# Turning q, k and alpha on VectorE instead of TensorE in a gated linear attention kernel

## The chip, the cores and the metric

The kernel runs on one core of a Trainium2 chip. The metric is the device time of one execution in microseconds (us). One run of the kernel before, at 390.9 us, was left out as slow. Engines are named as in the profile: PE is TensorE's matmuls, PEld its weight loads, DVE is VectorE, ACT is ScalarE, POOL is GpSimd, SP is SyncE; a "q" behind a name (SPq, ACTq) is that engine's sequencer, which issues the DMAs. "L102" is a line of the kernel's source.

## The reference

Two recurrences, one behind the other, all in fp32:

```python
# attention: batch 4, heads 8, steps S = 768, head width D = 48
for t in range(S):
    state = alpha[:, :, t, :, None] * state + einsum('bhd,bhe->bhde', k[:, :, t], v[:, :, t])
    y[:, :, t] = einsum('bhd,bhde->bhe', q[:, :, t], state)
x = y.transpose(0, 2, 1, 3).reshape(B, S, H * D)          # (4, 768, 384)

# gated state-space layer: d_model 384, d_inner 512
val, gate = split(x @ w_in)
for t in range(S):
    h = exp(A_log) * h + val[:, t, :]
    ys[:, t, :] = h
out = (silu(gate) * ys) @ w_out
```

## The kernel before

The kernel works in 12 groups n of 256 steps, three to a batch entry. The program of a group is cut into generators (`front` for the decays and scores, `back` for the attention output, `ssm` for the layer behind it), whose steps are dealt out by hand, so that TensorE works on group n's front, group n-1's back and group n-2's and n-3's layer in turn. In the timelines shown here each engine takes its instructions in that order.

Alpha, q and k arrive with the steps on the partitions. The recurrence is written with cumulative products of alpha along the steps, so all three must stand the other way round, channels on partitions and steps along the row. TensorE turns them, 128x128 at a time, into PSUM (`turned`):

```python
def front(n):
    ...
    def turned(name, jj):
        tp = ps_tp.tile([C, 2, GC], FP32, tag="tp", name="tp")
        for u in range(2):
            j = 2 * jj + u
            for c in range(G):
                nc.tensor.transpose(tp[:, u, ds(c * C, C)], pad[name][:, c, 2 * j:2 * j + 2, :], ident)
        return tp

    for jj in range(NP // 2):                  # alpha: scans V (backwards) and P (forwards)
        tp = turned("a", jj)
        ...
            nc.vector.tensor_tensor_scan(out=V[:, 2 * jj + u, GC - 1::-1], data0=tp[:, u, ::-1], ...)
        nc.vector.reciprocal(iV0[:, js], V[:, js, 0])
            nc.vector.tensor_tensor_scan(out=P[:, 2 * jj + u, :], data0=tp[:, u, :], ...)
    junk = p1.tile([C, NP, GC], FP32, name="junk")      # two range checks of V, on ScalarE
    nc.scalar.activation(junk, V[:, :, 0:GC], AF.Relu, ..., accum_out=left[:, n, 0:1])
    nc.scalar.activation(junk, V[:, :, 0:GC], AF.Relu, ..., accum_out=left[:, n, 1:2])
    yield
    ...     nc.vector.tensor_mul(Q[:, js], turned("q", jj), P[:, js])
    yield
    ...     nc.vector.tensor_mul(K[:, js], turned("k", jj), V[:, js, 1:GC + 1])
    yield
    ...     # scores sc = K.T Q on TensorE, masked into A by copy_predicated
```

The layer's two kinds of PSUM tile share two buffers (one tag), and the output copies are on ScalarE, behind the range checks in its order:

```python
def ssm(n, xT, prev_h, pool, ps_mm):           # ps_mm: 2 buffers
    for cc in range(NI):
        pj = ps_mm.tile([C, 2, GC], FP32, tag="mm", name="pj")
        ...                                     # pj = w_in.T xT; scan hh; sg = silu; f = sg * hh
        yield
    for c in range(G):
        o = ps_mm.tile([C, DM], FP32, tag="mm", name="o")
        ...                                     # o = f.T w_out
        nc.scalar.activation(o_sb, o, AF.Copy)
        nc.sync.dma_start(out=out[b, ds(g * GC + c * C, C), :], in_=o_sb)
        yield
```

A general version for data outside the range that the checks allow follows in the program; it is not taken for these inputs.

Of the kernel before, what the change touches and what calls it, by code (L numbers as in the profile page):

```python
# [10 lines left out]
U8 = mybir.dt.uint8  # L11
# [7 lines left out]
def kernel(  # L19
# [58 lines left out]
    def load_heads(dst, src, n, queue=nc.sync):  # L78

        b, g = divmod(n, NG)  # L80
        for c in range(G):
            rows = ds(g * GC + c * C, C)
            queue.dma_start(out=dst[:, c, :, 0:D], in_=src[b, :, rows, :].rearrange("h p d -> p h d"))  # L83

    def ssm(n, xT, prev_h, pool, ps_mm):
# [18 lines left out]
# [3 lines that stand above are left out]
                nc.tensor.matmul(o, f[:, cc, ds(c * C, C)], w_out[:, cc, :],  # L107
                                 start=(cc == 0), stop=(cc == NI - 1))
            o_sb = pool.tile([C, DM], FP32, name="o_sb")
            nc.scalar.activation(o_sb, o, AF.Copy)  # L110
            nc.sync.dma_start(out=out[b, ds(g * GC + c * C, C), :], in_=o_sb)
            yield
# [9 lines left out]
    def block_states(Kn, v_sb, pool, tag):  # L122

        z = pool.tile([C, NR, 512], FP32, tag=tag, name="z")
        zv = z[:, :, 0:GP * D].rearrange("p r (g j e) -> p r g j e", g=G, e=D)
        for g in range(G):
            for j in range(NP):
                for r in range(NR):
                    for i in range(2):
                        rows, chs = ds(R * r, R), ds(DP * i, DP)  # L130
                        nc.tensor.matmul(zv[chs, r, g, j, :], Kn[rows, g, j, chs],  # L131
                                         v_sb[rows, g, 2 * j + i, :], start=True, stop=True,
                                         skip_group_check=True)
        return zv

    def values_inside(A, v_sb, ps_y, pool, turn):
# [4 lines left out]
        for c in range(G):  # L141
            for j in range(NP):
                for r in range(NR):
                    for i in range(2):
                        rows, at = ds(R * r, R), ds(R * ((r + turn * i) % NR), R)
                        nc.tensor.matmul(yv[at, i, c, j, :], A[rows, i, c * NP + j, :],  # L146
                                         v_sb[rows, c, 2 * j + i, :],
                                         start=(c == 0 and j == 0), stop=False, skip_group_check=True)
# [32 lines left out]
    def ranged(ctx):  # L181
# [7 lines left out]
        wst = pool("wst", 1)  # L189
# [8 lines left out]
        pads = [{n: own.tile([C, G, H, DP], FP32, name=f"{n}_pad{i}") for n in "aqk"} for i in range(NBUF)]  # L198

        def clear_pads(i, name):  # L200
            nc.gpsimd.memset(pads[i][name][:, :, :, D:DP], 1.0 if name == "a" else 0.0)
# [3 lines left out]
        def load(n, names="aqkv", queue=nc.sync):  # L205
            for name in names:
                if name == "v":
                    vs[n] = p3.tile([C, G, H, D], FP32, name="v_sb")
                dst = vs[n] if name == "v" else pads[n % NBUF][name]
                load_heads(dst, dict(a=alpha, q=q, k=k, v=v)[name], n, queue)  # L210
# [10 lines left out]
        words, scales = [], {}  # L221

        def fetch_unit(u, queue=nc.sync):
            dst, src = units[u]
            m, w = dst.shape[1:]
            bits = wst.tile([C, m, w, 2], U32, name=f"bits{u}")
# [51 lines left out]
        def front(n):  # L278

            pad = pads[n % NBUF]  # L280
            V = Vs[n % 2]
            iV0 = p2.tile([C, NP], FP32, name="iV0")
            P = p1.tile([C, NP, GC], FP32, name="P")
            Q = p3.tile([C, NP, GC], FP32, name="Q")
            K = p2.tile([C, NP, GC], FP32, name="K")
# [4 lines left out]
            def turned(name, jj):  # L290
                tp = ps_tp.tile([C, 2, GC], FP32, tag="tp", name="tp")
                for u in range(2):
                    j = 2 * jj + u
                    for c in range(G):
                        nc.tensor.transpose(tp[:, u, ds(c * C, C)], pad[name][:, c, 2 * j:2 * j + 2, :], ident)  # L295
                return tp

            for jj in range(NP // 2):
                tp = turned("a", jj)
                js = slice(2 * jj, 2 * jj + 2)  # L300
                for u in range(2):
# [9 lines left out]
            junk = p1.tile([C, NP, GC], FP32, name="junk")  # L311
# [4 lines left out]
            yield  # L316
            for jj in range(NP // 2):
                js = slice(2 * jj, 2 * jj + 2)
                nc.vector.tensor_mul(Q[:, js], turned("q", jj), P[:, js])  # L319
            yield  # L320
            for jj in range(NP // 2):
                js = slice(2 * jj, 2 * jj + 2)
                nc.vector.tensor_mul(K[:, js], turned("k", jj), V[:, js, 1:GC + 1])  # L323
# [17 lines left out]
        def back(n):  # L341
# [20 lines left out]
            x_sb = p2.tile([C, G, DM], FP32, name="x_sb")  # L362
            xv = x_sb.rearrange("p g (j i e) -> p i (g j) e", i=2, e=D)
            ys = yv.rearrange("p i g j e -> p i (g j) e")
# [49 lines left out]

        with tc.manual_schedule():
            for n in range(N + 3):
# [16 lines left out]
                if n + 2 < N:  # L433
                    load(n + 2)
# [12 lines left out]
                step(new)  # L447
                if n == N:
# [6 lines left out]
    def general(ctx):  # L455
# [14 lines left out]
        pad = {n: p1.tile([C, G, H, DP], FP32, name=f"g{n}_pad") for n in "aqk"}  # L470
        for t in pad.values():
            nc.gpsimd.memset(t[:, :, :, D:DP], 0.0)
# [22 lines left out]
        for n in range(N):  # L495
            first = n % NG == 0
            for dst, src in (("a", alpha), ("q", q), ("k", k)):
                load_heads(pad[dst], src, n)
# [7 lines left out]
            for name in "aqk":  # L506
                for c in range(G):
                    ts = ds(c * C, C)
                    tp = ps_tp.tile([C, NP, C], FP32, tag="tp", name="tp")
                    for j in range(NP):  # L510
                        nc.tensor.transpose(tp[:, j, :], pad[name][:, c, 2 * j:2 * j + 2, :], ident)
# [9 lines left out]
            nc.gpsimd.tensor_mul(qk, pad["q"][:, :, :, 0:D], pad["k"][:, :, :, 0:D])  # L521
# [52 lines left out]
            for i in range(2):  # L574
                nc.vector.tensor_add(
                    x_sb.rearrange("p g (j i e) -> p i (g j) e", i=2, e=D)[:, i],
                    yv[:, i].rearrange("p g j e -> p (g j) e"),
                    qk.rearrange("p g (j i) e -> p i (g j) e", i=2)[:, i])
# [40 lines left out]
```

## Time and profile before

| | before |
|---|---|
| time, median of 3 runs (range) | 352.44 us (352.06 to 352.87) |
| span of the profiled run | 350.7 us |
| one group, first state matmul z to the next | 24.74 us |
| time without a gap on TensorE | 75 to about 303 us |

The page gives busy time by engine and in 40 slices; the chain of waits, the waits by line and the timeline say who holds up whom. The lines of these that carry the argument are in the prediction below. Two further views of the kernel before are wanted for comparison. First the row of one group in the table of stretches, whose columns are start and end, length, then busy time (and instructions) of PE, PEld, DVE, ACT and POOL, then the granted TensorE clock, the DMA share and GB/s:

```profile
155.09:179.83 24.74, 24.74 (x360) 20.18 (x359) 14.75 (x27) 8.27 (x18) 0.00 (x0) 1.00 0.46 81
```

TensorE is busy for the whole period; VectorE has 10 us to spare.

### The profile page before, as it was taken

What the parts mean: (1) busy time and instruction counts of PE and PEld (TensorE: products, weight loads), DVE (VectorE), ACT (ScalarE), POOL (GpSimd) and SP (SyncE); (2) the same over time, 40 slices, a digit from 0 to 9 for tenths busy, and PEclk for the clock granted to TensorE, in tenths of its full rate; (3) what the DMA queues carried; (4) which work ended last, traced back from release to release, by engine and by line L of the source; (5) the groups of instructions that cost most, each with busy time, mean ns of one, the idle gap of its engine ahead of it and who ended that gap; (6) DMA issues with size and microseconds to landing.
All of it is one profiled execution on the core that took longest, in us unless ns stands there. A gap on an engine that the chain in (4) does not pass through costs nothing.

```text
span 350.7 us, 9637 instructions
## 1 busy us (share of the span) xinstructions
PE 311.7 (89%) x4233; PEld 251.7 (72%) x4233; DVE 201.1 (57%) x373; ACT 113.4 (32%) x243; POOL 57.9 (17%) x77
## 2 busy tenths in 40 slices
PE   2445763899999999999999999999999999998994
PEld 1334652687887887887878878868878878776682
DVE  2939968567449448546566476384494485313140
ACT  1514564332324233313314324333342233222111
POOL 4388898640000000000000000000000000000000
PEclk9996585999999999999999999999999999999999
DMA  9999995440850921902904905908301010010101
GB/s 128 216 228 192 288 190 71 79 57 2 150 79 2 186 42 48 170 13 64 163 3 99 129 2 116 113 2 165 64 12 36 2 47 2 2 48 0 49 0 53
DMA packets 107650, 29.02 MB, mean 83 GB/s; under 512 B 100944, under 2 KB 107088, under 8 KB 107600
## 3 DMA queue, kind: packets, MB, share of 16 engines
q1 hardware_dynamic: 104992, 27.93, 45.1%
q10 hardware_dynamic: 2608, 0.40, 1.0%
q8 instruction: 35, 0.57, 0.7%
q14 instruction: 15, 0.12, 0.1%
HBM read 23.60 MB, written 4.72 MB: 81 GB/s over the span
## 4 chain that ended last, share of the span: by engine, by line
PE 80%; POOL 5%; SPq 5%; DVE 3%; DMA 3%; issue 3%; ACT 0%; POOLq 0%; DVEq 0%; ACTq 0%
PE pj L93 36%; PE o L107 18%; PE tp L295 7%; SPq L83 4%; PE z L131 4%; PE y L164 3%; PE sc L332 3%; PE y L146 3%; DMA bits<-in_moe_w_in_dram 3%; PE tpk L119 2%; PE tpx L173 2%; POOL ex L241 2%; SPq L227 1%; POOL w_in L251 1%; POOL w_in L250 1%
## 5 line engine op out<-in xcount | busy, mean ns | idle before, releaser
L93 PE MATMUL pj<-xT,w_in 128*128 128x256 f32 x576 | 134.2, 384 | 0.0
L93 PEld LDWEIGHTS pj<-xT,w_in 128*128 128x128 f32 x576 | 106.2, 190 | 14.2
L107 PE MATMUL o<-w_out,f 128*128 128x384 f32 x192 | 65.0, 492 | 0.0
L96 DVE TENSOR_TENSOR_SCAN hh<-a_dec,hh,pj 128x256 f32<-128x256 f32 x32 | 23.9, 747 | 68.5 <-PE pj L93 68.5
L101 ACT ACTIVATE sg<-pj 128x256 f32<-128x256 f32 x48 | 18.4, 384 | 119.9 <-DVE hh L96 119.9
L107 PEld LDWEIGHTS o<-w_out,f 128*128 128x128 f32 x192 | 35.5, 190 | 23.0 <-DVE f L102 0.5
L348 POOL TENSOR_TENSOR S_n<-S_end,V 128x192 f32<-128x192 f32 x8 | 4.3, 542 | 209.6 <-DVE S_end L357 209.6
L102 DVE TENSOR_TENSOR f<-sg,hh 128x256 f32<-128x256 f32 x48 | 20.9, 435 | 23.8 <-ACT sg L101 23.8
L307 DVE TENSOR_TENSOR_SCAN P<-tp,iV,bias 128x256 f32<-128x256 f32 x48 | 33.4, 738 | 0.8
L302 DVE TENSOR_TENSOR_SCAN V<-tp,bias 128x256 f32<-128x256 f32 x48 | 30.1, 670 | 5.1 <-PE tp L295 5.1
L312 ACT ACTIVATE junk<-V,bias 128x1024 f32<-128x1024 f32 x12 | 13.8, 1148 | 53.9 <-DVE V L302 53.9
L295 PE MATMUL tp<-ident,q_pad 128*128 128x128 f32 x96 | 15.4, 305 | 14.5 <-DVE P L307 7.8
L295 PE MATMUL tp<-ident,a_pad 128*128 128x128 f32 x96 | 14.6, 300 | 14.2 <-issue 6.6
L295 PEld LDWEIGHTS tp<-ident,q_pad 128*128 128x128 f32 x96 | 12.4, 157 | 18.9 <-issue 16.3
L96 DVE TENSOR_TENSOR_SCAN hh<-a_dec,pj 128x256 f32<-128x256 f32 x16 | 11.0, 685 | 25.8 <-PE pj L93 25.8
L295 PEld LDWEIGHTS tp<-ident,a_pad 128*128 128x128 f32 x96 | 12.4, 154 | 16.0 <-issue 7.0
L241 POOL TENSOR_SCALAR ex<-ex 128x384 uint32<-128x384 uint32 x12 | 18.5, 1543 | 16.6 <-DVE ex L236 16.2
L332 PEld LDWEIGHTS sc<-Q,K 64*64 64x64 f32 x768 | 14.3, 148 | 4.3 <-issue 3.0
L335 DVE COPY_PREDICATED A<-mask,sc 128x512 f32<-128x512 uint8 x24 | 16.0, 721 | 1.1 <-PE sc L332 1.1
L332 PE MATMUL sc<-Q,K 64*64 64x64 f32 x768 | 16.1, 237 | 0.5 <-DVE K L323 0.5
L146 PEld LDWEIGHTS y<-v_sb,A 64*64 64x64 f32 x768 | 13.8, 149 | 2.7 <-issue 2.7
L295 PE MATMUL tp<-ident,k_pad 128*128 128x128 f32 x96 | 14.5, 299 | 1.4 <-DVE Q L319 1.0
(60 smaller groups left out, 325.0 us busy)
## 6 DMA issues: line engine op xcount, KB each, us to landing
a_pad<-in_alpha_dram SPq DMA_DIRECT2D x24, 192.0 KB, 4.6
k_pad<-in_k_dram SPq DMA_DIRECT2D x24, 192.0 KB, 5.5
v_sb<-in_v_dram SPq DMA_DIRECT2D x24, 192.0 KB, 5.0
out_dram<-o_sb SPq DMA_DIRECT2D x24, 192.0 KB, 2.3
q_pad<-in_q_dram SPq DMA_DIRECT2D x22, 192.0 KB, 5.0
bits<-in_moe_w_in_dram SPq DMA_DIRECT2D x8, 384.0 KB, 5.1
bits<-in_moe_w_out_dram SPq DMA_DIRECT2D x4, 384.0 KB, 7.2
q_pad<-in_q_dram ACTq DMA_DIRECT2D x2, 192.0 KB, 5.5
```

The lines of the kernel that those rows point to most:

```text
L93: nc.tensor.matmul(pj[:, i, :], w_in[:, kk, i, ds(cc * C, C)], xT[:, kk, :], start=(kk == 0), stop=(kk == NK - 1))
L96: nc.vector.tensor_tensor_scan(out=hh, data0=a_dec[:, cc:cc + 1].to_broadcast([C, GC]), data1=pj[:, 0, :], initial=prev_h[cc][:, GC - 1:GC ...
L101: nc.scalar.activation(sg, pj[:, 1, :], AF.Silu)
L102: nc.vector.tensor_mul(f[:, cc, :], sg, hh)
L107: nc.tensor.matmul(o, f[:, cc, ds(c * C, C)], w_out[:, cc, :], start=(cc == 0), stop=(cc == NI - 1))
L146: nc.tensor.matmul(yv[at, i, c, j, :], A[rows, i, c * NP + j, :], v_sb[rows, c, 2 * j + i, :], start=(c == 0 and j == 0), stop=False, skip ...
L241: nc.gpsimd.tensor_scalar(out=ex, in0=ex, scalar1=896.0, scalar2=1151.0, op0=ALU.max, op1=ALU.min)
L295: nc.tensor.transpose(tp[:, u, ds(c * C, C)], pad[name][:, c, 2 * j:2 * j + 2, :], ident)
L302: nc.vector.tensor_tensor_scan(out=V[:, 2 * jj + u, GC - 1::-1], data0=tp[:, u, ::-1], data1=bias[:, 1:2].to_broadcast([C, GC]), initial=1 ...
L307: nc.vector.tensor_tensor_scan(out=P[:, 2 * jj + u, :], data0=tp[:, u, :], data1=bias[:, 1:2].to_broadcast([C, GC]), initial=iV0[:, 2 * jj ...
L332: nc.tensor.matmul(scv[ds(R * r, R), i, c * NP + j, :], K[rows, j, steps], Q[rows, j, steps], start=True, stop=True, skip_group_check=True)
L335: nc.vector.copy_predicated(out=A[:, i].rearrange("p x t -> p (x t)"), mask=mask[:, ds(i * GP * R, GP * R)], data=sc[:, i])
```

## The change

The intent is to take the transposes of alpha, q and k off the engine that is always busy. From the fifth group on (n = 4 to 11), a whole batch entry of the three (for n = 4 and 5 the part of it that is left) is loaded in 32-step squares, so that VectorE's transpose, one instruction for each of the three and each group (128x1024), finishes the turn in SBUF. The loads come as shorter runs on SP's queue; v loads and output stores go to ScalarE's queue, so that SP's long lists do not hold them up. The first four groups, the scans, the checks, the order of steps and the shared PSUM buffers stay. The core of it:

```diff
-            nc.sync.dma_start(out=out[b, ds(g * GC + c * C, C), :], in_=o_sb)
+            nc.scalar.dma_start(out=out[b, ds(g * GC + c * C, C), :], in_=o_sb)
...
+        BY_VECTOR = NG + 1
+        W = 32
+        def load_batch(b):
+            t = big.tile([C, 3, NP * NW * W], FP32, tag=f"big{1 - b % 2}", name="batch")
+            for m, (name, src) in enumerate((("a", alpha), ("q", q), ("k", k))):
...
+                            nc.sync.dma_start(
+                                out=tv[ds(DP * i + W * half, W), j * NW + w0:(j + nj) * NW, 0:ch],
+                                in_=src[b, ds(NP * i + j, nj), w0 * W:S, ds(W * half, ch)]
+                                .rearrange("j (w p) d -> p (j w) d", p=W))
...
+            def squares(name, dst):
+                nc.vector.transpose(dst, batches[b, name][:, :, ds(g * GC, GC)])
+            if by_vector:
+                aT = p1.tile([C, NP, GC], FP32, name="aT")
+                squares("a", aT)
             for jj in range(NP // 2):
-                tp = turned("a", jj)
+                tp = aT[:, js] if by_vector else turned("a", jj)
...
             yield
+            if by_vector:
+                squares("q", Q)
...
-                nc.vector.tensor_mul(Q[:, js], turned("q", jj), P[:, js])
+                nc.vector.tensor_mul(Q[:, js], Q[:, js] if by_vector else turned("q", jj), P[:, js])
             yield
+            if by_vector:
+                squares("k", K)
...
-                nc.vector.tensor_mul(K[:, js], turned("k", jj), V[:, js, 1:GC + 1])
+                nc.vector.tensor_mul(K[:, js], K[:, js] if by_vector else turned("k", jj), V[:, js, 1:GC + 1])
...
+                if n in starts:                          # {2: 1, 3: 2, 5: 3}
+                    load_batch(starts[n])
+                if NG <= n < N - 2:
+                    load(n + 2, "v", nc.scalar)
```

Cut: heads are paired j and j+4 instead of 2j and 2j+1 (so the loads of the first groups are cut in two), and buffers are re-used to make room (weight staging under a batch, Q and x_sb with one buffer fewer, junk in 8 bits).

More of the change, by code (lines that the diff above doesn't have):

```diff
@@ L82, in load_heads, with load_pairs @@
             rows = ds(g * GC + c * C, C)
-            queue.dma_start(out=dst[:, c, :, 0:D], in_=src[b, :, rows, :].rearrange("h p d -> p h d"))
+            queue.dma_start(out=dst[:, c], in_=src[b, :, rows, :].rearrange("h p d -> p h d"))
+    def load_pairs(dst, src, n, queue=nc.sync):
+        b, g = divmod(n, NG)
+        for c in range(G):
+            rows = ds(g * GC + c * C, C)
+            for i in range(2):
+                queue.dma_start(out=dst[:, c, :, i, 0:D],
+                                in_=src[b, ds(NP * i, NP), rows, :].rearrange("h p d -> p h d"))
     def ssm(n, xT, prev_h, pool, ps_mm):
@@ L131, in block_states @@
                         nc.tensor.matmul(zv[chs, r, g, j, :], Kn[rows, g, j, chs],
-                                         v_sb[rows, g, 2 * j + i, :], start=True, stop=True,
+                                         v_sb[rows, g, NP * i + j, :], start=True, stop=True,
                                          skip_group_check=True)
@@ L146, in values_inside @@
                         nc.tensor.matmul(yv[at, i, c, j, :], A[rows, i, c * NP + j, :],
-                                         v_sb[rows, c, 2 * j + i, :],
+                                         v_sb[rows, c, NP * i + j, :],
                                          start=(c == 0 and j == 0), stop=False, skip_group_check=True)
@@ L188, in ranged @@
         p3 = pool("p3", 3)
-        wst = pool("wst", 1)
+        big = pool("big", 1)
         wex = pool("wex", 3)
@@ L197, in ranged @@
         NBUF = 2
-        pads = [{n: own.tile([C, G, H, DP], FP32, name=f"{n}_pad{i}") for n in "aqk"} for i in range(NBUF)]
+        held = big.tile([C, NBUF, 3, G * H * DP], FP32, tag="big1", name="pads")
+        pads = [{n: held[:, i, m].rearrange("p (c j i d) -> p c j i d", c=G, j=NP, d=DP)
+                 for m, n in enumerate("aqk")} for i in range(NBUF)]
         def clear_pads(i, name):
-            nc.gpsimd.memset(pads[i][name][:, :, :, D:DP], 1.0 if name == "a" else 0.0)
+            nc.gpsimd.memset(pads[i][name][..., D:DP], 1.0 if name == "a" else 0.0)
+        BY_VECTOR = NG + 1
+        W = 32
+        NW = S // W
+        batches = {}
+        def load_batch(b):
+            t = big.tile([C, 3, NP * NW * W], FP32, tag=f"big{1 - b % 2}", name="batch")
+            for m, (name, src) in enumerate((("a", alpha), ("q", q), ("k", k))):
+                tv = t[:, m].rearrange("p (x e) -> p x e", e=W)
+                batches[b, name] = t[:, m].rearrange("p (j x) -> p j x", j=NP)
+                w0 = max(0, BY_VECTOR - NG * b) * GC // W
+                for i in range(2):
+                    nc.gpsimd.memset(tv[ds(DP * i + W, W), :, D - W:W], 1.0 if name == "a" else 0.0)
+                for j, nj in [(0, NP)] if w0 == 0 else [(j, 1) for j in range(NP)]:
+                    for i in range(2):
+                        for half in range(2):
+                            ch = min(W, D - W * half)
+                            nc.sync.dma_start(
+                                out=tv[ds(DP * i + W * half, W), j * NW + w0:(j + nj) * NW, 0:ch],
+                                in_=src[b, ds(NP * i + j, nj), w0 * W:S, ds(W * half, ch)]
+                                .rearrange("j (w p) d -> p (j w) d", p=W))
         vs, st, xs = {}, {}, {}
@@ L208, in load @@
                     vs[n] = p3.tile([C, G, H, D], FP32, name="v_sb")
-                dst = vs[n] if name == "v" else pads[n % NBUF][name]
-                load_heads(dst, dict(a=alpha, q=q, k=k, v=v)[name], n, queue)
+                    load_heads(vs[n], v, n, queue)
+                elif n < BY_VECTOR:
+                    load_pairs(pads[n % NBUF][name], dict(a=alpha, q=q, k=k)[name], n, queue)
         units = []
@@ L221, in ranged @@
         words, scales = [], {}
+        staging = big.tile([C, len(units), NK * C * 2], U32, tag="big0", name="staging")
         def fetch_unit(u, queue=nc.sync):
@@ L225, in fetch_unit @@
             m, w = dst.shape[1:]
-            bits = wst.tile([C, m, w, 2], U32, name=f"bits{u}")
+            bits = staging[:, u].rearrange("p (m w two) -> p m w two", m=m, two=2)
             queue.dma_start(out=bits.rearrange("p a n two -> p a (n two)"), in_=src.bitcast(U32))
@@ L280, in front @@
             pad = pads[n % NBUF]
+            b, g = divmod(n, NG)
+            by_vector = n >= BY_VECTOR
             V = Vs[n % 2]
@@ L283, in front @@
             P = p1.tile([C, NP, GC], FP32, name="P")
-            Q = p3.tile([C, NP, GC], FP32, name="Q")
-            K = p2.tile([C, NP, GC], FP32, name="K")
+            Q = p2.tile([C, NP, GC], FP32, name="Q")
+            K = p1.tile([C, NP, GC], FP32, name="K")
             A = As[n % 2]
@@ L294, in turned @@
                     for c in range(G):
-                        nc.tensor.transpose(tp[:, u, ds(c * C, C)], pad[name][:, c, 2 * j:2 * j + 2, :], ident)
+                        nc.tensor.transpose(tp[:, u, ds(c * C, C)], pad[name][:, c, j], ident)
                 return tp
+            def squares(name, dst):
[3 more added lines that the diff above has]
+                squares("a", aT)
             for jj in range(NP // 2):
-                tp = turned("a", jj)
                 js = slice(2 * jj, 2 * jj + 2)
+                tp = aT[:, js] if by_vector else turned("a", jj)
                 for u in range(2):
@@ L310, in front @@
                                                  op0=ALU.mult, op1=ALU.max)
-            junk = p1.tile([C, NP, GC], FP32, name="junk")
+            junk = p1.tile([C, NP, GC], U8, name="junk")
             nc.scalar.activation(junk, V[:, :, 0:GC], AF.Relu, scale=-1.0 / LOW, bias=bias[:, 0:1],
@@ L361, in back @@
             values_before(yv, s["Q"], S_n, first, 1)
-            x_sb = p2.tile([C, G, DM], FP32, name="x_sb")
-            xv = x_sb.rearrange("p g (j i e) -> p i (g j) e", i=2, e=D)
-            ys = yv.rearrange("p i g j e -> p i (g j) e")
+            x_sb = p1.tile([C, G, DM], FP32, name="x_sb")
+            xv = x_sb.rearrange("p g (i f) -> p i g f", i=2)
+            ys = yv.rearrange("p i g j e -> p i g (j e)")
             nc.scalar.activation(xv[:, 0], ys[:, 0], AF.Copy)
@@ L412, in any_outside @@
             nc.vector.tensor_scalar(out=flag, in0=w1, scalar1=0.0, scalar2=None, op0=ALU.is_gt)
+        starts = {2: 1, 3: 2, 5: 3}
         with tc.manual_schedule():
@@ L433, in ranged @@
                 if n + 2 < N:
-                    load(n + 2)
+                    load(n + 2, "aqkv" if n < NG else "aqk")
                 if n == 0:
@@ L469, in general @@
         ps_mm = pool("gs_mm", 2, space=PS)
-        pad = {n: p1.tile([C, G, H, DP], FP32, name=f"g{n}_pad") for n in "aqk"}
+        pad = {n: p1.tile([C, G, NP, 2, DP], FP32, name=f"g{n}_pad") for n in "aqk"}
         for t in pad.values():
-            nc.gpsimd.memset(t[:, :, :, D:DP], 0.0)
+            nc.gpsimd.memset(t[..., D:DP], 0.0)
         masks = {}
@@ L497, in general @@
             for dst, src in (("a", alpha), ("q", q), ("k", k)):
-                load_heads(pad[dst], src, n)
+                load_pairs(pad[dst], src, n)
             v_sb = p2.tile([C, G, H, D], FP32, name="v_sb")
@@ L510, in general @@
                     for j in range(NP):
-                        nc.tensor.transpose(tp[:, j, :], pad[name][:, c, 2 * j:2 * j + 2, :], ident)
+                        nc.tensor.transpose(tp[:, j, :], pad[name][:, c, j], ident)
                     if name == "a":
@@ L520, in general @@
             dg = p1.tile([C, G, H], FP32, name="dg")
-            nc.gpsimd.tensor_mul(qk, pad["q"][:, :, :, 0:D], pad["k"][:, :, :, 0:D])
+            for c in range(G):
+                nc.gpsimd.tensor_mul(qk[:, c].rearrange("p (i j) d -> p j i d", i=2), pad["q"][:, c, :, :, 0:D],
+                                     pad["k"][:, c, :, :, 0:D])
             nc.vector.tensor_reduce(out=dg, in_=qk, axis=mybir.AxisListType.X, op=ALU.add)
@@ L574, in general @@
             for i in range(2):
-                nc.vector.tensor_add(
-                    x_sb.rearrange("p g (j i e) -> p i (g j) e", i=2, e=D)[:, i],
-                    yv[:, i].rearrange("p g j e -> p (g j) e"),
-                    qk.rearrange("p g (j i) e -> p i (g j) e", i=2)[:, i])
+                f = ds(i * NP * D, NP * D)
+                nc.vector.tensor_add(x_sb[:, :, f], yv[:, i].rearrange("p g j e -> p g (j e)"),
+                                     qk.rearrange("p g h e -> p g (h e)")[:, :, f])
             xT = p1.tile([C, NK, GC], FP32, name="gxT")
```

## The prediction

> **What bounds the kernel now.** I first read busy time and the 40 slices on the page, then the stretches of 25 us, then one group's period in the timeline, engine by engine.
>
> ```profile
> PE 311.7 (89%) x4233; PEld 251.7 (72%) x4233; DVE 201.1 (57%) x373; ACT 113.4 (32%) x243; POOL 57.9 (17%) x77
> ...
> PE   2445763899999999999999999999999999998994
> ...
> PEclk9996585999999999999999999999999999999999
> ```
>
> The first 75 us (weight conversion, slices 1 to 8) have gaps on TensorE; from then to about 303 us it is solid, and the chain of waits runs along it. In the stretches from 75 to 300 us it is busy 25.00 of every 25 us. All eight changed groups (n = 4 to 11, from about 105 to 303 us) lie there. One group takes 24.74 us (first state matmul z at 155.09, the next at 179.83). What removing TensorE work is worth depends on who would be the next to keep it waiting, so here is TensorE's, VectorE's and ScalarE's order within that period (start, duration, engine, line, work, idle before it):
>
> ```profile
> 161.43 1.04 PE L295 MATMUL tp<-ident,q_pad 128*128 128x128 f32 x8
> 162.40 1.15 PE L146 MATMUL y<-v_sb,A 64*64 64x48 f32 x64
> 163.47 2.86 PE L93 MATMUL pj<-xT,w_in 128*128 128x256 f32 x12
> 166.17 1.04 PE L295 MATMUL tp<-ident,k_pad 128*128 128x128 f32 x8
> 167.13 1.15 PE L164 MATMUL y<-S_n,Q 64*64 64x48 f32 x64
> 168.21 2.86 PE L93 MATMUL pj<-xT,w_in 128*128 128x256 f32 x12
> 171.00 1.16 PE L332 MATMUL sc<-Q,K 64*64 64x64 f32 x64
> ```
>
> ```profile
> 155.52 0.43 DVE L102 TENSOR_TENSOR f<-sg,hh 128x256 f32<-128x256 f32 x1 [0.51 <-ACT sg L101]
> 155.86 1.26 DVE L302 TENSOR_TENSOR_SCAN V<-tp,bias 128x256 f32<-128x256 f32 x2
> ...
> 162.48 1.28 DVE L319 TENSOR_TENSOR Q<-tp,P 128x512 f32<-128x512 f32 x2
> 166.37 0.75 DVE L96 TENSOR_TENSOR_SCAN hh<-a_dec,hh,pj 128x256 f32<-128x256 f32 x1 [2.61 <-PE pj L93]
> ...
> 167.91 1.28 DVE L323 TENSOR_TENSOR K<-tp,V 128x512 f32<-128x512 f32 x2
> ```
>
> ```profile
> 159.95 1.15 ACT L312 ACTIVATE junk<-V,bias 128x1024 f32<-128x1024 f32 x1 [4.46 <-DVE V L302]
> ...
> 161.22 1.16 ACT L314 ACTIVATE junk<-V,bias 128x1024 f32<-128x1024 f32 x1
> ...
> 162.37 0.85 ACT L110 ACTIVATE o_sb<-o 128x384 f32<-128x384 f32 x2
> 163.61 0.17 ACT L151 ACTIVATE fence<-y 128x2 f32<-128x2 f32 x1 [0.39 <-PE y L146]
> ```
>
> What to see: the alpha scans V start the moment f is issued, so VectorE, not the alpha transposes, already times them. ScalarE's two range checks (junk) follow the scans, and only behind them, in ScalarE's fixed order, come the copies o_sb. The first pj matmuls of the group reuse the PSUM buffer that the first o_sb empties: two buffers are shared by o and pj. The first copy ends about 162.37 + 0.48 = 162.85; pj begins at 163.47. That hidden path (f, scans, checks, o_sb, pj) has only some 0.5 us of slack, though no wait shows on it.
>
> [...] The trace has no transpose on VectorE; its 128x512 products take 682 ns[...]. [...] the granted clock is 0.50 from 25.4, 35.5 and 52.7 us on, in the last two after under 2 us idle among small matmuls; but an idle stretch from 322.7 to 324.7 us among large ones leaves it at 1.00.
>
> **The change, part by part.**
>
> Removed: 24 transposes a group on TensorE. By distance between starts the eight of q take 0.97 us (161.43 to 162.40), of k 0.96, of alpha 0.97: 2.90 us a group, 23.2 us over eight groups. That is the ceiling (329 us), reached only if nothing else waits.
>
> Added on VectorE: three transposes a group, 3 x 1.22 = 3.7 us. VectorE is busy 14.9 of 24.74 us, so the sum fits (18.6), but the order decides. Count from the end of the last pj (154.12, where alpha's transposes start).
> - Before: V starts at 1.74, checks at 5.83, o_sb at 8.25, its first half done 8.72, pj at 9.35, K done at 15.07, sc at 16.88, last pj done at 24.74.
> - After: the alpha square takes V's place at 1.74; with 1.22 and a handover of 0.03, V starts at 2.99, the checks at 7.08, o_sb at 9.50, its first half done at 9.98, pj at about 10.1. TensorE is ready at 9.35 - 0.97 - 0.97 = 7.41, so it stands idle about 2.7 us: a new wait that eats both the alpha and the q transposes, and 0.75 more.
> - Behind pj the k transposes are gone: by TensorE alone sc comes at 16.88 + 0.75 - 0.96 = 16.67. But K now waits for hh (13.0), f (start to K's start 1.54), the k square 1.25 and two products 1.28: done at 17.07, its first half at 16.4; sc runs from 16.7 to 17.1 on. From sc to the last pj nothing changes (7.86).
> - New period: 24.6 to 25.0 us in place of 24.74. The q square lies in VectorE's idle 2.61 us.
> Over eight groups: -1 to +2 us; I take +0.5. The gain is nearly all lost.
>
> Loads: q, k and alpha come as runs of 128 and 64 bytes in place of 192: 98,304 packets in place of 49,152 for these groups. At the mean of queue q1 (45.1% of 16 x 350.7 us over 104,992 packets = 24 ns), a whole batch entry of 36,864 is 55 us of all 16 engines for three groups (74 us): it fits, with the v loads. But the built program has eight completion semaphores that all loads and stores use in turn, and each DMA waits for the earlier one on its semaphore. So the squares' loads are tied to ScalarE's queue: the last three k loads of the first batch wait for the stores of n = 4. These are issued at about 10 and 11.5 us in that group, land at about 13 and 14.5 (0.77 to issue, 2.3 to land), and the last k load lands near 18.5, where VectorE wants k at 14.5: about 3.8 us once. The second batch's last two k loads wait for the v loads at the end of n = 5, landing near 16.5: about 2 us once. Sum 5.8 us, part perhaps hidden.
>
> ScalarE: two stores and two v loads a group at 0.77 us of issue each (two stores took 1.54 on SP). The fence moves from behind o_sb to about 12.4, needed at 12.9: just in time, 0.5 us in all for late ones. Unchanged: converting the weights (loads of the first groups are cut in two, same packets, DMA full there anyway), the tail from 303 us, and the renamed head order.
>
> Clock: the idle 2.7 us follow 1.1 us of 64x64 matmuls. [...] If half the groups pay 1.4 us, that is 5.6 us; I give it an even chance: 2.8.
>
> Sum: 352.4 + 0.5 + 5.8 + 0.5 + 2.8 = 362.0 us.
>
> **The rivals.**
> - TensorE stays the bound and takes the whole 23 us (329 to 335 us). For: it is busy all the time, VectorE only 57%. Against: the 0.5 us of slack at o_sb. It needs a VectorE transpose well under 0.5 us, twice.
> - VectorE becomes the bound: should fp32 squares run at half rate (2.3 us), V and K move by 1.1 each, the period goes to about 27.2, and the time to 372 to 378. No row of the trace excludes it[...].
> - DMA becomes the bound: at 55 us a batch entry and a shared chain of semaphores, ScalarE could stand behind a load that is late, and every engine with it: 5 to 15 us more. The DMA share of 0.45 before speaks against it as a steady state.
> - Parity: squares at 1.1 us, loads in time, no clock loss: 351 to 353 us.
>
> **Range and chances.** Parity with the one-off waits gives 352 to 358, the clock 358 to 367, half-rate squares up to 376. Predicted 362, 351 to 376 eight times in ten. Faster by over 2% (under 345.4) needs a period under 23.9, which my path excludes unless the square takes about 0.5 us: 0.06. Within 2%: 0.38. Slower (over 359.5): 0.56.
>
> **What would show it.** In the changed profile: transposes on VectorE of about 1.2 us; TensorE's pj waiting about 2.7 us on o_sb once a group, TensorE busy well under 25 of 25 us; period near 24.8; VectorE's k square waiting for DMA at n = 4 and n = 6; clock digits under 9 past 105 us. Wrong if pj does not wait on ScalarE, if the squares take 0.6 us or 2.3 us, or if ScalarE's queue stalls in a load's issue.

Passages that rested on no trace or run of this case are cut out of the prediction, their places marked. The sum on record came to 362.0 us and stands with all its terms, but the working of two of them is cut. The 1.22 us of a VectorE transpose, which the +0.5 us rests on, are the author's estimate; a straight line through VectorE's products in the trace of the kernel before (0.435 us for 128x256, L102; 0.682 us for 128x512, L319) gives 1.18 us for 128x1024, an estimate too. That half the groups pay 1.4 us, in the 2.8 us for the clock, is a guess, which that trace does not show.

## More of the kernel before

Second, of TensorE's waits, the two kinds that matter for the comparison; all of its waits lie outside the stretch from 75 to 303 us (total, times, longest):

```profile
PE y L164 <- ACT fence L151: 1.1, 2, 0.6
...
PE sc L332 <- DVE K L323: 0.5, 1, 0.5
```

TensorE never waits for an output copy `o_sb`, and hardly for K.

## The result

| | before | after |
|---|---|---|
| median of 4 runs each (range) | 352.65 us (352.06 to 354.24) | 363.04 us (361.24 to 363.68) |
| ratio, 95% interval | | 1.0279 (1.0226 to 1.0332): slower |
| span of the profiled run | 350.7 us | 360.6 us |

Here and below a ratio is the mean time of one kernel's fast runs over that of the other's of the same rounds, so not quite the ratio of the medians quoted.

From the page of the kernel after: busy times, TensorE's 40 slices and its granted clock.

```profile
PE 302.2 (84%) x4041; PEld 236.3 (66%) x4041; DVE 231.1 (64%) x397; ACT 114.0 (32%) x243; POOL 82.5 (23%) x95
...
PE   2445955899997897997997997997989979998894
...
PEclk9999995999998998799999998999998999999999
```

TensorE has 192 instructions fewer and is busy for 9.5 us less, yet the run is 10 us longer. Where the row of slices was a solid 9 there is now a dip in every group, and the clock digits fall under 9 past 105 us. What it waits for, past the first groups, is in the list of TensorE's waits:

```profile
PE pj L102 <- ACT o_sb L119: 19.5, 8, 2.5
...
PE sc L381 <- DVE K L372: 2.0, 2, 1.5
```

The first line, absent before, comes eight times, once in each changed group; of the second, 1.5 us fall in n = 4 and 0.5 us in the first groups, as before. Here is that wait in the timeline of a regular group, n = 6, which begins with z at 160.49 (start, duration, engine, line, work; in brackets the idle time before it and its releaser), first TensorE, then VectorE, then ScalarE:

```profile
160.49 1.15 PE L140 MATMUL z<-v_sb,Kn 64*64 64x48 f32 x64
161.57 5.43 PE L116 MATMUL o<-w_out,f 128*128 128x384 f32 x16
166.93 1.15 PE L155 MATMUL y<-v_sb,A 64*64 64x48 f32 x64
170.45 2.86 PE L102 MATMUL pj<-xT,w_in 128*128 128x256 f32 x12 [2.38 <-ACT o_sb L119]
```

```profile
161.79 0.42 DVE L111 TENSOR_TENSOR f<-sg,hh 128x256 f32<-128x256 f32 x1 [0.51 <-ACT sg L110]
162.14 1.24 DVE L338 STREAM_TRANSPOSE aT<-batch 128x1024 f32<-128x1024 f32 x1
163.41 1.27 DVE L347 TENSOR_TENSOR_SCAN V<-aT,bias 128x256 f32<-128x256 f32 x2
```

```profile
167.51 1.15 ACT L357 ACTIVATE junk<-V,bias 128x1024 uint8<-128x1024 f32 x1 [5.75 <-DVE V L347]
...
168.78 1.15 ACT L359 ACTIVATE junk<-V,bias 128x1024 uint8<-128x1024 f32 x1
...
169.93 0.47 ACT L119 ACTIVATE o_sb<-o 128x384 f32<-128x384 f32 x1
```

Read the three together. The alpha square sits between f and the first scan V, where before the scan began at once. Everything behind it, the second pair of scans, the two checks and the copy o_sb, moves back by its 1.24 us. At the same time the alpha and q transposes have left TensorE, which is ready for pj at 168.07. The PSUM buffer that pj needs comes free with o_sb at 170.40, and pj starts at 170.45.

By group, in the table of stretches (same columns as above):

```profile
104.70:132.88 28.18, 24.16 (x319) 18.62 (x318) 18.99 (x31) 8.28 (x18) 0.51 (x1) 0.94 0.88 86
132.88:160.49 27.61, 25.17 (x336) 19.38 (x335) 18.69 (x31) 8.37 (x18) 8.74 (x7) 0.88 1.02 92
160.49:185.23 24.74, 22.36 (x335) 17.45 (x335) 18.36 (x30) 8.31 (x18) 0.00 (x0) 1.00 1.07 104
185.23:210.04 24.81, 22.37 (x320) 17.45 (x319) 18.78 (x31) 8.28 (x18) 0.52 (x1) 1.00 0.91 98
210.04:236.47 26.43, 23.99 (x336) 18.58 (x335) 18.58 (x31) 8.37 (x18) 0.51 (x1) 0.94 0.49 61
236.47:261.22 24.75, 22.36 (x336) 17.46 (x335) 18.35 (x30) 8.32 (x18) 0.00 (x0) 1.00 0.13 34
261.22:287.71 26.49, 24.05 (x320) 18.55 (x319) 18.77 (x31) 8.28 (x18) 0.51 (x1) 0.94 0.12 31
287.71:312.45 24.74, 22.30 (x336) 17.46 (x335) 18.58 (x31) 8.37 (x18) 0.52 (x1) 1.00 0.05 18
```

Four groups (n = 6, 7, 9, 11) take 24.74 to 24.81 us, what a group took before: TensorE does 2.38 us less and waits 2.38 us. The other four take 26.4 to 28.2 us, and they are exactly the four whose granted clock is under 1.00. In n = 4 and n = 5 the timeline shows the burst of pj behind the gap running slowly, 4.54 us and 5.49 us where it is 2.86 at full clock:

```profile
142.91 5.49 PE L102 MATMUL pj<-xT,w_in 128*128 128x256 f32 x12 [2.44 <-ACT o_sb L119]
```

Group n = 4 has one more wait, for k's loads, which were issued last of the batch (VectorE, then TensorE):

```profile
122.53 1.25 DVE L338 STREAM_TRANSPOSE K<-batch 128x1024 f32<-128x1024 f32 x1 [1.56 <-DMA batch<-in_k_dram]
```

```profile
124.65 1.44 PE L381 MATMUL sc<-Q,K 64*64 64x64 f32 x64 [1.49 <-DVE K L372]
```

The sum: the eight periods of the kernel after are 207.75 us, 9.75 more than eight of 24.75. Of this 1.5 us is the late k of n = 4, and what is left, 8.3 us, is in the four groups with the lower clock (1.9, 2.9, 1.7 and 1.7 us). The four groups at full clock give nothing back and cost nothing. Start and end of the run differ by less than 1 us.

### The profile page after: what moved, and what is told of

It is laid out like the page before. It is cut to its first block, busy times and chain, and to the rows that moved or that the text cites. A ratio compares the mean times of both kernels' runs of the same rounds, so it can differ in the third digit from the quotient of the medians.

```text
span 360.6 us, 9318 instructions
## 1 busy us (share of the span) xinstructions
PE 302.2 (84%) x4041; PEld 236.3 (66%) x4041; DVE 231.1 (64%) x397; ACT 114.0 (32%) x243; POOL 82.5 (23%) x95
## 4 chain that ended last, share of the span: by engine, by line
PE 49%; DVE 17%; DMA 9%; SPq 7%; ACT 6%; issue 6%; POOL 3%; ACTq 1%; DVEq 0%; POOLq 0%
PE pj L102 32%; DVE V L347 6%; PE o L116 4%; DVE P L352 4%; PE sc L381 3%; PE y L173 3%; SPq L233 3%; ACT junk L357 3%; DMA staging<-in_moe_w_in_dram 3%; PE tpx L182 3%; DVE aT L338 2%; PE tpk L128 2%; SPq L91 2%; DVE hh L105 2%; DMA out_dram<-o_sb 2%
## 5 line engine op out<-in xcount | busy, mean ns | idle before, releaser
L102 PE MATMUL pj<-xT,w_in 128*128 128x256 f32 x576 | 142.3, 401 | 19.5 <-ACT o_sb L119 19.5
L102 PEld LDWEIGHTS pj<-xT,w_in 128*128 128x128 f32 x576 | 111.6, 200 | 36.4 <-ACT o_sb L119 20.4
L116 PEld LDWEIGHTS o<-w_out,f 128*128 128x128 f32 x192 | 35.5, 190 | 23.0 <-DVE f L111 0.5
L334 PE MATMUL tp<-ident,pads 128*128 128x128 f32 x96 | 20.1, 364 | 28.8 <-issue 14.5
L334 PEld LDWEIGHTS tp<-ident,pads 128*128 128x128 f32 x96 | 15.0, 184 | 33.1 <-issue 24.4
L228 POOL MEMSET batch<- 32x1536 f32 x18 | 24.7, 1372 | 46.4 <-DVE K L338 35.7
L357 ACT ACTIVATE junk<-V,bias 128x1024 uint8<-128x1024 f32 x12 | 13.8, 1148 | 65.2 <-DVE V L347 59.4
L352 DVE TENSOR_TENSOR_SCAN P<-aT,iV,bias 128x256 f32<-128x256 f32 x32 | 22.3, 739 | 0.6
L347 DVE TENSOR_TENSOR_SCAN V<-aT,bias 128x256 f32<-128x256 f32 x32 | 20.2, 673 | 0.3
L119 ACT ACTIVATE o_sb<-o 128x384 f32<-128x384 f32 x24 | 11.6, 483 | 18.4 <-PE o L116 14.0
L173 PEld LDWEIGHTS y<-S_n,Q 64*64 64x64 f32 x704 | 13.4, 143 | 5.3 <-issue 4.4
```

The costliest lines, as they stand in the source:

```text
L102: nc.tensor.matmul(pj[:, i, :], w_in[:, kk, i, ds(cc * C, C)], xT[:, kk, :], start=(kk == 0), stop=(kk == NK - 1))
L116: nc.tensor.matmul(o, f[:, cc, ds(c * C, C)], w_out[:, cc, :], start=(cc == 0), stop=(cc == NI - 1))
L173: nc.tensor.matmul(yv[at, i, c, j, :], Q[rows, j, ds(R * x, R)], S_n[rows, x, j, :], start=False, stop=(c == G - 1 and j == NP - 1), skip_ ...
L228: nc.gpsimd.memset(tv[ds(DP * i + W, W), :, D - W:W], 1.0 if name == "a" else 0.0)
L357: nc.scalar.activation(junk, V[:, :, 0:GC], AF.Relu, scale=-1.0 / LOW, bias=bias[:, 0:1], accum_out=left[:, n, 0:1])
```

## The experiments

The theory: the 2.4 us gap at pj is the path f, alpha square, scans, checks, o_sb; it returns all that TensorE was spared; the rest of the loss is the clock, halved by the same gap, and one late load. The rivals: VectorE's order behind pj (hh, f, k square, K) is the limit anyway; the DMA and its queues are; the halved clock has a cause of its own. All ten kernels gave right results. Each was timed in four runs; 'before' is that of the same call, medians 353.28, 353.01 and 352.77 us. Kernels of different calls ran on different chips, so they are compared by their ratios.

### Checks behind the output copies (checks_late)

```diff
+            yield
             junk = p1.tile([C, NP, GC], U8, name="junk")
             nc.scalar.activation(junk, ..., accum_out=left[:, n, 0:1])
             nc.scalar.activation(junk, ..., accum_out=left[:, n, 1:2])
-            yield
```

> The changed kernel with ScalarE's two range checks moved behind the o_sb copies and their stores; nothing else. My theory: the 2.4 us wait of pj on o_sb (8 times, 19.5 us) vanishes, since o_sb no longer stands behind the alpha square, the scans and the checks; the next limit is K (square, scans, q square, hh, k square, products), which holds sc for about 2 us, so a period of about 24.0 us without clock losses; the k loads of n = 4 come in time because the stores are issued 6 us earlier. About 346 us, up to 354 if the clock still halves behind the new gap at sc. Rival, VectorE or the loads as the bound: no gain, 360 or more, and the idle time of TensorE stays the same in sum. Rival, parity: equal to the kernel before only if TensorE has no gap at all, which would be about 330.

Measured: 353.45 us (350.58 to 354.99), ratio 0.9974 (0.9916 to 1.0032). The wait of pj for o_sb is gone from the list of TensorE's waits, and another has come:

```profile
PE sc L381 <- DVE K L372: 16.4, 9, 3.7
```

The path by the checks is therefore the one that held pj, as the theory says. But freeing it only brings the run back to where it was before the change. In the five groups at full clock the period goes to between 23.9 and 24.4 us, no lower because sc now waits for K (1.45 to 1.91 us each). In the other three (n = 4, 5 and 11) the clock fell (in stretches of 25 us it is 0.93 to 0.97 from 100 to 175 us, 1.00 from there to 275 us, and 0.94 from 275 to 300 us), and they take 26.0 to 27.4 us. The late k load of n = 4 did not go away, against the expectation: sc waits 3.7 us there. The rival was right to this extent: VectorE's order is the next limit, close behind.

### The same in the kernel before (before_checks_late)

The same edit, on the kernel before.

> Control: the kernel before with the same move of the range checks. Theory: TensorE is solid there and nothing waits on o_sb, so nothing changes: 352 to 353 us. If it gets faster, the hidden path through the checks was already on the chain before.

Measured: 353.2 us (352.82 to 353.48), ratio 0.9996 (0.9974 to 1.0019). Moving the checks is worth nothing where TensorE is always busy, so what it gives in checks_late and in squares_early below is not a gain that the old kernel missed; it is the wait that the change made.

### The gap filled with matmuls (fill and fill5)

These put matmuls that nobody reads into the gap, to keep TensorE busy without moving any other engine:

```diff
             yv = values_inside(s["A"], v_sb, ps_y, p2, 1)
+            if n + 1 >= BY_VECTOR and n + 1 < N:
+                spare = ps_tp.tile([C, GC], FP32, tag="tp", name="spare")
+                for _ in range(10):          # fill5: range(5)
+                    nc.tensor.matmul(spare, w_in[:, 0, 0, 0:C], w_in[:, 0, 1, 0:GC], start=True, stop=True)
             yield
```

> The changed kernel with ten idle-time matmuls (128x128 by 128x256, result unused, into a free PSUM buffer) put between y and pj in groups 4 to 11, where TensorE waits 2.4 us: 80 more matmuls. Theory, the half clock follows the light stretch of about 3.6 us: the clock stays at 1.00 past 105 us, no pj burst takes 4.5 or 5.5 us any more, and the time falls by the 8 us that the trace shows for halved bursts (1.7 at n = 4, 2.7 at n = 5, 1.7 at n = 8 and 10): about 355 us. Rival, the half clock has another cause or TensorE has no room there: 363 us or up to 18 us more (80 times 0.22).

Measured: 367.76 us (367.18 to 368.5), ratio 1.0413 (1.0386 to 1.044). The dose was wrong. Ten such matmuls are twenty instructions and took 4.58 us, 2.2 us more than the gap; the period rose to some 26.6 us. The clock stayed at 1.00 from 100 us on, so the run supports the theory, but its time decides nothing. Half the dose fits:

> The run with idle-time matmuls again, at half the length: the trace of that run shows each such matmul as two instructions of 0.22 us, so ten of them took 4.4 us where 2.4 us were free, and the period became 26.6 us, with the clock at 1.00 throughout. Five take 2.2 us and fit. Theory, light stretches halve the clock: all periods but that of n = 4 near 24.8 us, no halved pj burst, clock 1.00 past 105 us, about 355 to 357 us. Rival, the clock is not tied to the gap: 361 to 364 as in the changed kernel, with halved bursts still there.

Measured: 355.45 us (354.98 to 358.51), ratio 1.0089 (1.0031 to 1.0147). From its page the clock, and from its timeline the filled gap:

```profile
PEclk9995596799999999999999999999999999999999
```

```profile
164.63 2.42 PE L412 MATMUL spare<-w_in 128*128 128x256 f32 x10
167.08 2.86 PE L102 MATMUL pj<-xT,w_in 128*128 128x256 f32 x12
```

Every pj burst behind the filled gap takes 2.86 us, the clock is whole past 70 us, and seven of the eight periods are 24.74 to 24.81 us (n = 4 is 26.3, with the late k). The kernel does 40 matmuls more than the kernel after and is 7.6 us faster by the medians, 6.7 us by the ratios (0.019 of 353; the ends of the two intervals leave 2.8 to 10.6 us). That is the halved clock of the kernel after, measured: the gap causes it, and by the middle values it accounts for most of the loss.

Why some groups are hit and others, with the same gap, are not, can be read from the granted clock in the table of stretches, taken in steps of 0.5 us. In the kernel after it is 0.50 from 115.0 to 118.4 us, 142.3 to 149.1, 220.8 to 224.2 and 272.0 to 275.4: all eight of these times lie on one grid of 3.41 us (from 115.0 to 275.4 us are 47 steps). At n = 4, 8 and 10 the whole gap (2.44 to 2.48 us) lies between two points of the grid, and the clock falls at the second. At n = 5, 1.83 us of the gap do, behind the 1.15 us of y. At n = 6, 7, 9 and 11 a point of the grid falls into the gap, at most 1.82 us lie on one side of it, with a part of o or pj, and the clock stays whole. A full-clock period of 24.74 us is 7.25 steps of the grid, so from group to group the gap moves a quarter of a step along it. So in this trace, between 100 and 300 us, the steps at full clock that half clock followed had 1.83, 2.44, 2.44 and 2.48 us of idle time in them, and no other had more than 1.82 us. That is no rule: from 22.9 to 26.2 us there was no matmul at all, and the clock stayed at 1.00 up to 53.5 us. In k_early and queue_sp, too, only some of the eight groups were hit: in their timelines the pj burst behind the gap takes 4.12 to 4.54 us in four and five of them, and 2.86 us in the others.

### Alpha's square one group ahead (alpha_early)

```diff
             if by_vector:
-                aT = p1.tile([C, NP, GC], FP32, name="aT")
-                squares("a", aT)
+                aT = early.pop((n, "a"))
...
                 nc.vector.copy_predicated(out=A[:, i]..., data=sc[:, i])
+            if BY_VECTOR <= n + 1 < N:
+                early[n + 1, "a"] = p1.tile([C, NP, GC], FP32, name="aT")
+                squares("a", early[n + 1, "a"], n + 1)
```

> The changed kernel with the square of alpha turned one group ahead, in VectorE's idle 1.6 us behind A, same work in sum. Theory: V starts 1.25 us earlier, so the wait of pj on o_sb falls from 2.4 to about 1.2 us, the light stretch is too short for the half clock, and the period falls by about 1.1 us to 23.6: 8 x 1.1 + 8 of clock less, some 346 to 349 us. Rival, VectorE's sum of work is the bound: unchanged, 361 to 364. Rival, the loads: unchanged, or slower as alpha is wanted earlier.

Measured: 349.12 us (347.83 to 349.46), ratio 0.9872 (0.984 to 0.9904). The wait is halved:

```profile
PE pj L102 <- ACT o_sb L119: 9.2, 8, 1.2
```

The regular period is 23.46 to 23.53 us, 1.3 less than after: the 1.24 us of the alpha square come off the period nearly one to one, as they must if it lies on the path that sets pj. Another 1.1 us of gap stays, as the checks are still ahead of o_sb; at that length the clock of the regular groups is 1.00 (in its stretches of 25 us from 150 to 300 us). The k loads of n = 4 come no sooner than in the kernel after (the k square starts at 122.70 us, there at 122.53) but are wanted sooner: sc waits 4.6 us for them, which takes back part.

### k's square ahead (k_early)

```diff
-            yield
             if by_vector:
                 squares("k", K)
+            yield
```

> The changed kernel with k's square alone moved ahead of the first hh. Theory: in a regular group sc is held by TensorE's own order behind the late pj, not by K, so the wait of pj on o_sb (8 times 2.4 us) stays and the time hardly moves: 360 to 364 us. Rival, K's path was the bound of the changed kernel: about 1 us a group less, under 355.

Measured: 362.64 us (360.61 to 363.5), ratio 1.0286 (1.0263 to 1.031), with the same wait of pj, 19.5 us in eight. The regular period falls by less than 0.2 us (to 24.57 to 24.63). So in the kernel as changed the k square is not what holds the group; the rival is wrong for the kernel after, though right behind it.

### The queues undone (queue_sp)

```diff
-            nc.scalar.dma_start(out=out[b, ds(g * GC + c * C, C), :], in_=o_sb)
+            nc.sync.dma_start(out=out[b, ds(g * GC + c * C, C), :], in_=o_sb)
...
-                    load(n + 2, "v", nc.scalar)
+                    load(n + 2, "v", nc.sync)
```

> Undoes the second part of the change alone: v loads and stores issued from SP again, squares as in the changed kernel. Theory: the cause of the slowdown is the order on VectorE and ScalarE, so pj still waits 2.4 us on o_sb eight times and the clock still halves in some groups; only the 1.5 us that sc waited at n = 4 for late k loads goes, since no load waits for a store of ScalarE's queue any more: 359 to 363 us. Rival, ScalarE's DMA issue is what costs: under 355. Rival, stores stuck behind the squares' loads in SP's queue: over 366, with o_sb waiting for a DMA.

Measured: 363.33 us (361.31 to 364.12), ratio 1.0272 (1.0229 to 1.0314): the same as after. The first batch's k loads were issued by 101.5 us instead of 119.8, and the wait for K in n = 4 is gone (the 0.5 us left lie in the first groups). The rival of the stores stuck behind the squares' loads came true once: at n = 5 the two copies o_sb waited 1.2 and 0.2 us for their buffers, pj waited 3.7 us there (20.7 us in all), and the clock fell in five groups instead of four. In this kernel the gain and the loss of the queue part cancel, so the DMA rival is out as the cause of the slowdown.

### All squares and the checks moved (all_early)

Everything above in one: alpha's and q's squares one group ahead, behind the scores' copies; k's before the products wait for hh; the checks behind o_sb. The same instructions as in the kernel after, in another order:

```diff
             if BY_VECTOR <= n + 1 < N:
                 early[n + 1, "a"] = p1.tile([C, NP, GC], FP32, name="aT")
                 squares("a", early[n + 1, "a"], n + 1)
+                early[n + 1, "q"] = p2.tile([C, NP, GC], FP32, name="Q")
+                squares("q", early[n + 1, "q"], n + 1)
```

(this on top of alpha_early, checks_late and k_early, with Q taken from `early` as aT is).

> The changed kernel with all three squares and the checks moved: alpha's and q's squares one group ahead, behind A; k's before the first hh; the checks behind o_sb. The same instructions, VectorE's sum unchanged. Theory: no wait of TensorE is left in a regular group, period 21.9 to 22.3 us (24.74 less 2.90), clock 1.00; at n = 4 the k loads come late by 6 us or more, as k is wanted 3 us earlier: 336 to 342 us. Rival, VectorE's sum binds (231 us busy, 85% in these periods): 345 or more, with waits of pj or sc on VectorE in each group.

Measured: **333.65 us** (333.0 to 334.31), ratio 0.9443 (0.9419 to 0.9466), 5.6% faster than before. The waits for o_sb are gone; of K's, one of 1.4 us at n = 4 is left. Its table of stretches:

```profile
150.00:175.00 25.00, 25.00 (x407) 19.71 (x405) 19.06 (x32) 9.43 (x22) 0.00 (x0) 1.00 1.01 107
175.00:200.00 25.00, 25.00 (x335) 19.17 (x328) 21.14 (x37) 8.53 (x19) 0.80 (x1) 1.00 0.62 87
200.00:225.00 25.00, 25.00 (x368) 18.90 (x368) 21.25 (x38) 9.04 (x20) 0.83 (x1) 1.00 0.47 75
```

TensorE is solid again at full clock, VectorE busy for 19 to 21 of 25 us, and the regular period is 22.10 to 22.13 us, 2.6 less than before. The change's own work was never too much for VectorE; it was put where it stood in the way. The first stretch has a DMA share of 1.01, and no engine waits for a DMA in it. The late k at n = 4 cost 1.45 us, less than expected; the k loads had all been issued by 113.6 us, 6 us sooner than in the kernel after. Why is not settled: the stores that share their semaphores also come sooner in this order.

### The same without the checks (squares_early)

all_early with the checks left ahead of o_sb.

> All three squares moved as in the fastest version, but the range checks left ahead of o_sb. Theory: o_sb's first half ends some 8.75 us into the group where TensorE is ready at 7.4, so pj waits 1.2 us in each group as in the run with only alpha early; K no longer matters; period 23.4 us, clock 1.00: 343 to 346 us, so the checks' place is worth about 10 us (8 x 1.25) of the fastest version's gain. Rival, the checks do not matter once the squares are early: 333 to 335.

Measured: 345.91 us (344.36 to 346.87), ratio 0.9794 (0.9761 to 0.9827). The wait of pj is 9.2 us in eight, 1.2 at most, as in alpha_early, and the regular period is 23.29 to 23.36. So the place of two activations of 1.15 us is worth 3.5% here (0.9794 against 0.9443), and 0.0% in the kernel before.

### The best order without the queues (all_early_sp)

all_early with v loads and stores back on SP, as in queue_sp.

> The same with v loads and stores issued from SP. Theory: the late k loads at n = 4 go too, since the first batch's loads then wait for no store: 331 to 336 us, 6 us less than with ScalarE's queue. Rival, the DMA engines' rate sets when k lands: as slow as with ScalarE's queue. Rival, stores behind the loads hold o_sb: slower than with ScalarE's queue.

Measured: 343.17 us (342.52 to 344.42), ratio 0.9729 (0.9702 to 0.9756), 9.5 us slower than all_early; the rival named in the expectation was right. One group, n = 5, took 32.6 us, and its timeline tells why (ScalarE, then TensorE):

```profile
142.37 0.49 ACT L119 ACTIVATE o_sb<-o 128x384 f32<-128x384 f32 x1 [14.09 <-DMA out_dram<-o_sb]
```

```profile
142.91 4.87 PE L102 MATMUL pj<-xT,w_in 128*128 128x256 f32 x12 [8.38 <-ACT o_sb L119]
```

The copy waits for its SBUF buffer, whose store stood on SP behind the second batch's loads (of ScalarE's 14.1 idle us some 11.6 are this wait, an estimate: the half of o that it copies was done at about 130.7, half way through the o matmuls of 128.02 to 133.45); pj waits 8.4 us for the copy and then runs at half clock. The queue part of the change is thus worth 9.5 us, but only in an order that has something to lose.

### Together

| kernel | median us | ratio to before | regular period us | what TensorE waits for in the changed groups, us |
|---|---|---|---|---|
| after | 363.04 | 1.0279 | 24.74 to 24.81 | o_sb 19.5, K 1.5 |
| fill5 | 355.45 | 1.0089 | 24.74 to 24.81 | K 1.3 (gap filled) |
| queue_sp | 363.33 | 1.0272 | | o_sb 20.7 |
| k_early | 362.64 | 1.0286 | 24.57 to 24.63 | o_sb 19.5, K 2.7 |
| checks_late | 353.45 | 0.9974 | 23.9 to 24.4 | K 15.9 |
| alpha_early | 349.12 | 0.9872 | 23.46 to 23.53 | o_sb 9.2, K 4.6 |
| squares_early | 345.91 | 0.9794 | 23.29 to 23.36 | o_sb 9.2, K 3.3 |
| all_early_sp | 343.17 | 0.9729 | | o_sb 8.4, once |
| all_early | 333.65 | 0.9443 | 22.10 to 22.13 | K 1.4 |

The waits for K are those of the lists less the 0.5 us in the first groups, and the regular period is that of groups at full clock. The other parts of the change (head order, re-used buffers, junk in 8 bits) were not run alone; all_early has them all and is 5.6% faster than before, so they are not what made the change slow.

## Why the prediction was right

The time, 363.04 us against 362.0: right, and so was the mechanism. The size of two terms was not: the loads were taken 4.3 us too long and the clock 5.5 us too short. That the sum came within about 1 us is luck.

- **"That hidden path (f, scans, checks, o_sb, pj) has only some 0.5 us of slack."** Right, and it decided everything. Counted in group n = 6 from where TensorE goes on behind the last pj (now z, at 160.49), the square begins at 1.65, V at 2.92, the checks at 7.02, o_sb at 9.44 and pj at 9.96: each 0.06 to 0.14 us earlier than counted out beforehand. checks_late and alpha_early show it to be the cause.
- **"TensorE stands idle about 2.7 us."** 2.38 to 2.48 us. The step behind it, 2.90 us removed a group, was a little large: TensorE's work fell by 2.38 us in the regular group after, and by 2.63 us in all_early, where it is solid. So TensorE was ready for pj at 7.58 and not at 7.41. The remaining 0.27 us can be read by distance between starts in the two timelines: where a group of transposes went, what stood before it takes 0.09 us longer to the 64x64 matmuls that now follow (o 5.36 us for 5.27, pj 2.79 for 2.70, the last pj 2.68 for 2.59).
- **"Squares of 1.22 us."** 1.24. The rival of half rate, 2.3 us, is out.
- **"New period: 24.6 to 25.0 us."** 24.74 to 24.81. Over eight groups about +0.1 us, where +0.5 was taken.
- **"Late k loads, 5.8 us."** Mis-sized: 1.5 us. n = 4 lost 1.5 instead of 3.8, and the stall at n = 6 did not come at all (no wait for a load in its timeline). One part of the working was visibly too long: a store's issue on ScalarE took 0.36 us in all but one of the changed groups' stores, where 0.77 had been read from SP. Whether that explains the rest is not shown. The tie itself is real: in the trace of the kernel after all 181 DMAs tell of their landing on eight semaphores, and these are waits of SP's queue, where it issues the batches' loads (L233) and stands for v loads and stores that ScalarE issued.

```profile
SPq L233 <- DMA v_sb<-in_v_dram: 43.6, 5, 16.2
SPq L233 <- DMA out_dram<-o_sb: 27.9, 3, 12.7
```

- **"The fence, 0.5 us."** Nothing: the list of TensorE's waits has the fence with 1.1 us in two, the same as before.
- **"Clock: an even chance of 5.6 us, 2.8."** Mis-sized: 8.3 us by the periods, 6.7 to 7.6 by fill5. "Half the groups" was right in the profiled run (four of eight), but each cost 1.7 to 2.9 us where 1.4 was taken, and the even chance halved it again. At n = 4, 8 and 10, with 3.41 us at 0.50, the pj burst takes 1.68 us longer (4.54 us for 2.86). At n = 5 the clock stayed at 0.50 for 6.83 us. The idle time before a fall differs: in the last 3.41 us it was 1.83 us at n = 5, and in the kernel before 1.64 us ahead of the fall at 52.7 us and, in two parts of under 2 us, 2.79 us ahead of the one that the prediction puts at 35.5 us. Had the loads been as late as predicted, the run would have ended near 367 us.
- **The rivals.** TensorE as the bound, VectorE at half rate and DMA as the bound are excluded by the waits above. Parity, 351 to 353 us, is nearly where the kernel would be without the clock: 363.0 less 7.6 is 355.4, and the late k is 1.5 us of what is left.

What the prediction did not ask is whether the order could be mended. The same instructions in another order give 333.65 us, near the 329 us that it called the ceiling.

## What to carry to other kernels

Before taking work off the engine that bounds a kernel, find the path that would be the next to hold it, by counting each engine's own order up to the next shared buffer: a slack of 0.5 us, on which no wait showed, decided what became of 23 us of removed work. When work moves to an engine with time to spare, place it where that engine idles, ahead of need, not between a producer and its waiting consumer; and move what nobody waits for (here two checks) behind what somebody does. Count the clock with a regular short gap on TensorE: here gaps of 2.4 us cost 1.7 to 2.9 us more through it in four of eight groups.
